# Retention and feed-forward on one core: no limit on the loads under way, and other places for rows 8 to 11

## The chip, the cores and the metric

The kernel runs on one core of one Trainium2 chip. The metric is the device time of one execution in microseconds. The core has five engines that each take their own instructions in order: PE (matrix products; its weight loads are listed apart as PEld), DVE (vector), ACT (scalar), POOL and SP. SP issues nearly all DMA transfers here; 16 DMA engines carry them. SBUF is the memory on the core, PSUM the banks into which PE writes, HBM the large memory outside.

## What is computed

A retention layer (an attention whose state decays by a constant per head) is followed by a feed-forward layer with a hard-swish product. The reference, cut to what matters:

```python
# q, k, v: (4, 8, 768, 64); w_in: (512, 2048); w_out: (2048, 512)
gamma = 1.0 - 2.0 ** (-5.0 - np.arange(H, dtype=np.float32))
for t in range(S):
    state = gamma[None, :, None, None] * state + np.einsum('bhd,bhe->bhde', k[:, :, t], v[:, :, t])
    y[:, :, t] = scale * np.einsum('bhd,bhde->bhe', q[:, :, t], state)
x = y.transpose(0, 2, 1, 3).reshape(B * S, H * D)      # 3072 tokens x 512
h = x @ w_in
g = h * np.clip(h + 3.0, 0.0, 6.0) / 6.0
return g @ w_out
```

## The kernel before

**Tiling.** The 3072 tokens are 24 rows of 128. Four rows (one block of 128 time steps of each of the four batches) make a unit of 512 tokens, so there are six units. The kernel has two phases. In the first, the retention of a row gives a 128 x 512 piece of x; with the four pieces of a unit, sixteen tiles of the first feed-forward product follow, one for each block of 128 columns of `w_in`; each result `g` is written to HBM (`gd`). In the second phase (from about 300 us) `g` is read back and multiplied by `w_out`, in a form that needs seven products for eight. To keep float32 accuracy, each operand is split into a high and a low float32r part, and a product is made as high x high, high x low and low x high. One tile (`mm1_step`, line 654) is so twelve matmuls of 512 columns, and its `h` is turned into `g` by ACT (line 668) and DVE (line 671) and stored by SP (line 677).

**Weights.** `w_in` and `w_out` arrive as 64-bit words, and `convert` (line 197) makes float32 of a block of 128 x 512: SP fetches 512 KB into `st` (two buffers), ACT takes the absolute value (line 210), DVE clips, shifts and joins in four steps (lines 214, 218, 229, 235), then ACT and DVE split it into high and low (lines 261 and 165). In the first phase block j of `w_in` is needed by tile j of unit 0.

**A row.** Its four parts are `kt`, `qt`, `vn`, `kn`, 256 KB each. `load` (line 453) fetches them; `vn` is scaled by decays on ACT and POOL (rows 0 to 7: ACT line 474, for rows 0 to 3 half of it on POOL) or on POOL alone (line 471, later rows). PE then makes the scores (line 383), the product with the state carried over (line 371), the new state part (line 408) and, after DVE and ACT have masked the scores into `am` (lines 542 and 547), the inner product (line 395). DVE scales the result by `dq` (line 633) and ACT and DVE split it into x (lines 261 and 165). `burst(new, old)` (line 693) puts the scores and the state part of one row and the two `y` products of the row before it on PE together. Rows 0 to 7 have space of their own (`early`); for later rows the buffers `kt`, `kn` have one place each, `qt` and `vn` two.

**What sets the order.** PE's order is the order in which steps are added. The list `turns` (line 726) has four tiles of unit 0, then one tile of unit 0 and one of unit 1 in turn, then units 2 to 5. After each turn `advance(n)` adds bursts until n of them are there; of `retention`'s steps (line 706), the 11th is the first half of row 8, the 12th is row 9 with the second half of row 8, and so on to the 15th, row 12 with row 11. For unit 1 the line that says when is

```python
advance(2 * UR + 3 + int((jj + 1) / NF * UR + 0.5))
```

with UR = 4 and NF = 16: the 11th step behind the unit's first tile, the 12th to 15th behind its second, sixth, tenth and fourteenth (jj = 1, 5, 9, 13). On the other engines the class `Plan` (line 42) decides: each step has a cost, a rank and dependencies, and `order` (line 71) plays the program through and issues what could start first, by rank where several could. For a load it takes that it lands no sooner than FLIGHT after its issue, that transfers follow each other at RATE us for each KB, and that no load starts before the DEPTH-th last has landed. While SP still has loads of rank under -50 (the list FIRST, line 422: rows 0 to 7 and blocks 0 to 4 of `w_in`), it takes them in exactly that order. Where PE would stand idle in this play, in the first 60 us, `spin` (line 761) adds matmuls on a constant to keep PE running. The resulting order is written into the program; on the chip each engine keeps to it and waits where data come later.

**The limit.** `load_from` (line 187), used for rows, decays and weights, adds to each load a wait until the fourth load back has landed. The stores of `g` and the second phase's loads (line 812) do not use it.

Of the kernel before, what the change touches and what calls it, by code (L numbers as in the profile page):

```python
# [41 lines left out]
class Plan:  # L42


    SEEN = {"PE": 0.25, "DVE": 0.14, "ACT": 0.16, "POOL": 0.2, "SP": 0.0}
    FIRST, RATE, FLIGHT, DEPTH = 2.0, 0.00266, 2.0, 4

    def __init__(self):
        self.steps, self.boxes = [], {}
# [6 lines left out]
    def add(self, engine, cost, run, deps=(), rank=0.0, boxes=(), kb=0, port=False):  # L56
        step = Step(engine, cost, run, [d for d in deps if d], rank, self.SEEN[engine])
        step.kb, step.boxes, step.port = kb, boxes, port or engine == "POOL"
        for b in boxes:
            b.users.append(step)  # L60
        self.steps.append(step)
        return step
# [52 lines left out]
def retention_ffn(ctx: ExitStack, tc: tile.TileContext, qkv, w_in, w_out, dvs, dqs, out, B, H, S, D):  # L115
# [6 lines left out]
    nc = tc.nc  # L122
    DM, NT = out.shape
    NF = w_in.shape[0]
# [5 lines left out]
    UR = 4  # L130
# [50 lines left out]
    plan = Plan()  # L181
# [4 lines left out]

    def load_from(to, src):

        ins = nc.sync.dma_start(out=to, in_=src).ins  # L189
        if len(started) >= plan.DEPTH:  # L190
            tc.add_manual_dep(ins, started[-plan.DEPTH], behind, reason="few loads at a time")
        started.append(ins.name)

    behind = mybir.DependencyInfo(mybir.DependencyClass.Sync, mybir.DependencyReason.DATA)
    started = []

    def convert(src, rank, soon=None):

# [3 lines left out]
        def fetch():  # L202
            t["st"] = wst_tile("st", I64, 2)
            load_from(t["st"], src)
            words = t["st"].bitcast(I32).rearrange("p (n w) -> p n w", w=2)
            t["lo"], t["hi"] = words[:, :, 0], words[:, :, 1]
# [82 lines left out]
    def build_w1(j, rank):  # L289
        spans, k = [], 0  # L290
        while k < NK:
            s, o = divmod(j * NK + k, 14)
            spans.append((k, min(NK - k, 14 - o)))
            if s not in w1_boxes:
                w1_boxes[s] = place_box("w" if s else "w0")
            k += spans[-1][1]
        t, box, dep = convert(w_in[j], rank, first("w", j, rank - 3))

        def parts():
            w = t["w"].rearrange("p (k n) -> p k n", k=NK)  # L300
            for k, n in spans:
                to, o = w1_block(j, k)
                yield to[:, o : o + n, 0], to[:, o : o + n, 1], w[:, k : k + n]

        mine = [w1_boxes[(j * NK + k) // 14] for k, n in spans]
        w1_ready[j] = split_step(parts, [n * P for k, n in spans], dep, rank, (box, *mine)), mine
# [4 lines left out]
    def build_w2(n, rank):  # L311
        j, h = divmod(n, 2)
        if not h:
            w2_boxes[j] = place_box(W2[j])
        t, box, dep = convert(w_out[j, h], rank)
        sums = plan.box("ws", 1)

        def add_up():
            w = t["w"].rearrange("p (b n) -> p b n", b=4)
            t["sm"] = sm = wst.tile([P, 4, P], F32, tag="ws", name=nm("ws"))  # L320
            m12, m11, m21, m22 = (w[:, i] for i in range(4))
            dve_sub(sm[:, 1], m12, m11)
            dve_sub(sm[:, 3], m22, m12)
            dve_sub(sm[:, 2], m22, sm[:, 1])
            dve_sub(sm[:, 0], sm[:, 2], m21)

        def target():
            if j not in w2c:
                w2c[j] = place([P, 7, 2, 2, P], F32R, nm("w2"), W2[j])
            return w2c[j]  # L330

        def parts():
            to, w = target(), t["w"].rearrange("p (b n) -> p b n", b=4)
            yield to[:, 0:3, 0, h], to[:, 0:3, 1, h], w[:, 1:4]

        def more():
            to = target()
            yield to[:, 3:7, 0, h], to[:, 3:7, 1, h], t["sm"]

        both = add("DVE", 1.0, add_up, (dep,), rank, (box, sums), port=True)  # L340
        split_step(parts, [3 * P], dep, rank, (box, w2_boxes[j]))
        split_step(more, [4 * P], both, rank, (sums, w2_boxes[j]))
# [79 lines left out]
    FIRST = [(0, "vn"), ("w", 0), (0, "kt"), (0, "qt"), (0, "kn")]  # L422
# [10 lines left out]
    def load_part(x, src, o, rank):  # L433

        if o is not None:
            e, i = divmod(o, 7)
            if e not in early_boxes:
                early_boxes[e] = plan.box("wf" if e < 2 else "we", 2 if e < 2 else 3)
            box = early_boxes[e]
        else:  # L440
            box = plan.box(f"l{x}", BUFS[f"l{x}"])
        to = {}

        def fetch():
            if o is not None:
                to["t"] = early_tile(e)[:, i]
            else:
                to["t"] = apool.tile([P, NPAIR, P], F32, tag=f"l{x}", name=nm(x), bufs=BUFS[f"l{x}"])
            load_from(to["t"].rearrange("p h n -> p (h n)"), src)

        return to, box, add("SP", 0.35, fetch, tiles_done[-5:-4], rank, (box,), kb=256)
# [202 lines left out]
    def mm1_step(u, jj, at):  # L654
        h_box, g_box, t = plan.box("h", NH), plan.box("g", 3), {}

        def run():
            t["h"] = h = ps_h.tile([P, UT], F32, tag="h", name=nm("h"))
            for k in range(NK):
                w, o = w1_block(jj, k)  # L660
                for n, (a, b) in enumerate(((0, 0), (0, 1), (1, 0))):
                    nc.tensor.matmul(  # L662
                        h, w[:, o, a], xs[u][b][:, k], start=k + n == 0, stop=(k, n) == (NK - 1, 2), skip_group_check=True
                    )

        def upper():
            t["g"] = hpool.tile([P, UT], F32, tag="g", name=nm("g"))
            nc.scalar.activation(out=t["g"], in_=t["h"], func=AF.Relu, bias=three)  # L668

        def product():  # L670
            ins = nc.vector.scalar_tensor_tensor(  # L671
                out=t["g"], in0=t["g"], scalar=6.0, in1=t["h"], op0=ALU.min, op1=ALU.mult
            )
            ends.append(ins.ins)

        def store():
            nc.sync.dma_start(out=gd[jj // 2][:, u, jj % 2], in_=t["g"])

        ready, mine = w1_ready[jj]
        assert len(x_ready[u]) == UR  # L680
        one = add("PE", 2.72, run, (ready, *x_ready[u]), at, (h_box, *mine, *x_boxes[u]))
        tiles_done.append(one)
        two = add("ACT", 0.62, upper, (one,), at + 1, (h_box, g_box))
        three_ = add("DVE", 0.61, product, (two,), at + 1, (h_box, g_box))
        add("SP", 0.35, store, (three_,), at + 1, (g_box,), kb=256)
# [5 lines left out]
    at = iter(range(1 << 30))  # L691
# [27 lines left out]
    def advance(n):  # L719

        nonlocal done
        while done < min(n, NROW + 3):
            next(gen)
            done += 1
# [7 lines left out]
    for n, (u, jj) in enumerate(turns):  # L732
        while n_w1 < min(NF, jj + 2):
            build_w1(n_w1, next(at) + (W_NEXT if n_w1 else W_FIRST))
            n_w1 += 1
        if jj in WHEN.get(u, ()):
            build_w2(n_w2, next(at) + 6.0)
            n_w2 += 1
        if (u, jj) == (NU - 1, 0):
            add("PE", 0.0, lambda: swap_pools(), (), float(next(at)))  # L740
        mm1_step(u, jj, float(next(at)))
        if n < UR:
            advance(UR + 2 + n + (n == UR - 1))
        elif u == 1:
            advance(2 * UR + 3 + int((jj + 1) / NF * UR + 0.5))
        elif 1 < u < NU - 1:
            advance(UR * (u + 1) + 3 + int((jj + 1) / NF * UR + 0.5))

# [7 lines left out]
    def swap_pools():  # L756
        nonlocal late
        att.close()
        late = ctx.enter_context(tc.tile_pool(name="late", bufs=1, side="right", reuse_waits="tile"))
# [249 lines left out]
```

## Time and profile before

| | us |
|---|---|
| median of three runs | 587.72 |
| lowest and highest | 585.54, 588.31 |
| the profiled execution's own time | 588.53 |
| its span, first to last instruction | 586.7 |
| PE busy | 568.4 |
| DVE busy | 418.9 |
| ACT busy | 244.1 |

The page gives busy times for each engine, and the span in 40 slices with one digit for each slice (tenths of the slice that the engine was busy; PEclk is the granted clock of PE, also in tenths). A row of a timeline has the start, the duration, the engine, the line, and in square brackets the idle time before it and what ended it. A row of the waits says which instruction stood, what released it, the total, how often and the longest. A row with two numbers and a colon ahead is a stretch of the span, with the busy time of PE, its weight loads, DVE, ACT and POOL, the granted clock, the DMA engines' busy share, and GB/s.

The mean over the whole span hides the stages: PE's share is 97%, but the first slices differ from the rest.

### The profile page before, as it was taken

How to read it: one execution, taken by the hardware profiler on the slowest of the kernel's cores; microseconds unless marked ns; L12 is line 12 of the kernel's file. 1: busy time of each engine (PE TensorE's matmuls, PEld its weight loads, DVE VectorE, ACT ScalarE, POOL GpSimd, SP SyncE). 2: the span in 40 equal slices, each digit the busy share in tenths (PEclk: the TensorE clock that was granted, in tenths of full speed). 3: DMA queues.
4: the chain of work that ended last, by engine and by line, in shares of the span. 5: the costliest groups of instructions: out<-in, count | busy, mean ns of one | idle time of the engine just before them, and what ended most of it. 6: DMA issues, size and time to landing. Idle time of an engine off the chain costs nothing.

```text
span 586.7 us, 12760 instructions
## 1 busy us (share of the span) xinstructions
PE 568.4 (97%) x5102; PEld 467.7 (80%) x5102; DVE 418.9 (71%) x752; ACT 244.1 (42%) x442; POOL 20.9 (4%) x25
## 2 busy tenths in 40 slices
PE   7687999999999999999999999999999999999997
PEld 6566888888888888888888888888888888888885
DVE  3567898888943598443345967998689966799743
ACT  5464444544422343222234544444444344344330
POOL 1000000000010000000000000000000000000000
PEclk9899999999999999999999999999999999999999
DMA  8888557757654466455245529974789546897002
GB/s 269 251 262 285 197 190 262 250 173 258 232 205 157 168 218 233 155 193 176 92 161 185 189 94 332 384 240 121 238 285 306 177 113 190 278 320 227 1 1 107
DMA packets 61260, 119.91 MB, mean 204 GB/s; under 512 B 7057, under 2 KB 7313, under 8 KB 61201
## 3 DMA queue, kind: packets, MB, share of 16 engines
q1 hardware_dynamic: 60912, 119.04, 60.8%
q8 instruction: 40, 0.66, 0.5%
q14 instruction: 20, 0.16, 0.1%
q10 hardware_dynamic: 288, 0.06, 0.0%
HBM read 87.61 MB, written 31.46 MB: 203 GB/s over the span
## 4 chain that ended last, share of the span: by engine, by line
PE 90%; DMA 8%; DVE 1%; ACT 0%; issue 0%; SPq 0%; DVEq 0%; ACTq 0%
PE h L662 44%; PE o L848 40%; DMA early<-in_qkv 6%; DMA st<-in_w_in 3%; PE y L395 2%; PE sc L383 2%; PE y L371 1%; PE sc L408 1%; SPq L189 0%; ACT wm L210 0%; DVE am L542 0%; DVE wb L229 0%; ACT g L668 0%; ACT w L261 0%; DVE ww L235 0%
## 5 line engine op out<-in xcount | busy, mean ns | idle before, releaser
L662 PE MATMUL h<-x,w 128*128 128x512 f32 x1152 | 269.2, 393 | 0.8 <-DVE x L165 0.7
L662 PEld LDWEIGHTS h<-x,w 128*128 128x128 f32 x1152 | 215.1, 188 | 47.2 <-DVE x L165 1.1
L848 PE MATMUL o<-gc,w 128*128 128x512 f32 x1008 | 233.2, 393 | 0.0
L848 PEld LDWEIGHTS o<-gc,w 128*128 128x128 f32 x1008 | 189.3, 188 | 43.7
L671 DVE SCALAR_TENSOR_TENSOR g<-g,h 128x512 f32<-128x512 f32 x96 | 65.8, 685 | 82.1 <-ACT g L668 81.4
L668 ACT ACTIVATE g<-h,three 128x512 f32<-128x512 f32 x96 | 65.7, 686 | 113.0 <-PE h L662 112.8
L253 ACT ACTIVATE gc<-gr 128x512 fp32r<-128x512 f32 x120 | 71.5, 623 | 57.2 <-PE o L848 43.3
L165 DVE TENSOR_TENSOR gc<-gr,gc 128x512 fp32r<-128x512 f32 x120 | 79.3, 684 | 20.9 <-ACT gc L253 20.8
L253 ACT ACTIVATE gc<-keep 128x512 fp32r<-128x512 f32 x48 | 30.4, 632 | 64.4 <-PE o L848 42.2
L165 DVE TENSOR_TENSOR gc<-keep,gc 128x512 fp32r<-128x512 f32 x48 | 32.8, 685 | 12.6 <-ACT gc L253 12.5
L210 ACT ACTIVATE wm<-st 128x512 f32<-128x512 f32 x32 | 21.5, 672 | 39.8 <-DMA st<-in_w_out 19.8
L471 POOL TENSOR_TENSOR vn<-vn,cst_sb 128x512 f32<-128x512 f32 x16 | 18.2, 1137 | 245.1 <-DMA vn<-in_qkv 220.5
L261 ACT ACTIVATE x<-xr 128x512 fp32r<-128x512 f32 x24 | 15.1, 630 | 27.2 <-DVE xr L633 27.1
L214 DVE TENSOR_SCALAR wm<-wm 128x512 f32<-128x512 f32 x32 | 13.5, 422 | 15.8 <-ACT wm L210 15.7
L865 DVE SCALAR_TENSOR_TENSOR u<-o,u 128x512 f32<-128x512 f32 (+1 forms) x31 | 20.0, 664 | 6.4 <-PE o L848 6.4
L229 DVE SCALAR_TENSOR_TENSOR wb<-st,wb 128x512 int32<-128x512 int32 x32 | 23.3, 727 | 0.2
L235 DVE SCALAR_TENSOR_TENSOR ww<-st,wb 128x512 int32<-128x512 int32 x32 | 21.9, 686 | 0.3
L261 ACT ACTIVATE w<-ww 128x384 fp32r<-128x384 f32 (+2 forms) x34 | 18.5, 549 | 6.9 <-DVE ww L235 6.8
L168 DVE TENSOR_TENSOR keep<-gr,gr 128x512 f32<-128x512 f32 x24 | 16.4, 686 | 5.8 <-DMA gr<-gd 5.7
L165 DVE TENSOR_TENSOR w<-ww,w 128x384 fp32r<-128x384 f32 (+2 forms) x34 | 19.9, 590 | 0.7 <-ACT w L261 0.7
L542 DVE TENSOR_TENSOR am<-sc,mask 128x512 f32<-128x512 f32 (+1 forms) x26 | 16.5, 641 | 3.4 <-ACT am L547 2.2
L165 DVE TENSOR_TENSOR x<-xr,x 128x512 fp32r<-128x512 f32 x24 | 16.5, 687 | 3.1 <-ACT x L261 2.3
(52 smaller groups left out, 335.0 us busy)
## 6 DMA issues: line engine op xcount, KB each, us to landing
gr<-gd SPq DMA_DIRECT2D x168, 256.0 KB, 4.3
gd<-g SPq DMA_DIRECT2D x96, 256.0 KB, 2.6
early<-in_qkv SPq DMA_DIRECT2D x32, 256.0 KB, 4.5
st<-in_w_in SPq DMA_DIRECT2D x16, 512.0 KB, 4.2
st<-in_w_out SPq DMA_DIRECT2D x16, 512.0 KB, 3.9
kt<-in_qkv SPq DMA_DIRECT2D x16, 256.0 KB, 4.0
qt<-in_qkv SPq DMA_DIRECT2D x16, 256.0 KB, 4.3
vn<-in_qkv SPq DMA_DIRECT2D x16, 256.0 KB, 4.9
```

The lines of the kernel that those rows point to most:

```text
L165: return nc.vector.tensor_tensor(out=out_, in0=a, in1=b, op=ALU.subtract)
L210: nc.scalar.activation(out=t["m"], in_=t["hi"].bitcast(F32), func=AF.Abs)
L229: nc.vector.scalar_tensor_tensor(out=b, in0=t["hi"], scalar=-0x40000000, in1=b, op0=ALU.bitwise_and, op1=ALU.bitwise_or)
L235: nc.vector.scalar_tensor_tensor(out=t["w"].bitcast(I32), in0=t["lo"], scalar=29, in1=t["b"], op0=ALU.logical_shift_right, op1=ALU.bitwise_or,
L253: nc.scalar.activation(out=hi, in_=src, func=AF.Copy)
L261: nc.scalar.activation(out=hi, in_=src, func=AF.Copy)
L471: nc.gpsimd.tensor_tensor(out=v, in0=v, in1=scale[:, :, None].to_broadcast([P, hs.stop - hs.start, D]), op=ALU.mult)
L662: nc.tensor.matmul(h, w[:, o, a], xs[u][b][:, k], start=k + n == 0, stop=(k, n) == (NK - 1, 2), skip_group_check=True)
L668: nc.scalar.activation(out=t["g"], in_=t["h"], func=AF.Relu, bias=three)
L671: ins = nc.vector.scalar_tensor_tensor(out=t["g"], in0=t["g"], scalar=6.0, in1=t["h"], op0=ALU.min, op1=ALU.mult)
L848: nc.tensor.matmul(banks[b, i, h], w2c[jj][:, RIGHT[i], a, h], gc[:, q, c], start=jj == 0 and n == 0, stop=jj == NFP - 1 and n == 2, skip_ ...
L865: nc.vector.scalar_tensor_tensor(out=out_[:, cut], in0=banks[b, i, h][:, cut], scalar=f, in1=other[:, cut], op0=ALU.mult, op1=ALU.add)
```

## The change

The limit in `load_from` goes, with the list that it kept; the planner's constants become FLIGHT 2.2 and DEPTH 9; and for unit 1 the bursts are put behind other tiles.

```diff
-    FIRST, RATE, FLIGHT, DEPTH = 2.0, 0.00266, 2.0, 4
+    FIRST, RATE, FLIGHT, DEPTH = 2.0, 0.00266, 2.2, 9
...
     def load_from(to, src):

-        ins = nc.sync.dma_start(out=to, in_=src).ins
-        if len(started) >= plan.DEPTH:
-            tc.add_manual_dep(ins, started[-plan.DEPTH], behind, reason="few loads at a time")
-        started.append(ins.name)
-
-    behind = mybir.DependencyInfo(mybir.DependencyClass.Sync, mybir.DependencyReason.DATA)
-    started = []
+        nc.sync.dma_start(out=to, in_=src)
...
         if n < UR:
             advance(UR + 2 + n + (n == UR - 1))
         elif u == 1:
-            advance(2 * UR + 3 + int((jj + 1) / NF * UR + 0.5))
+            advance(2 * UR + 3 + sum(jj >= x for x in (4, 7, 10, 13)))
```

With the new line the 11th step stays behind the first tile of unit 1; the 12th to 15th come behind its fifth, eighth, eleventh and fourteenth (jj = 4, 7, 10, 13). The loads of a row are added with its burst and wait for the fifth-last tile step added by then, so they move along.

## The prediction

> **What bounds the kernel now.** I read the slices of the whole span first, then who PE waited for, then the busy time by stage, then SP's waits and the landing times. The page's slices:
>
> ```profile
> PE   7687999999999999999999999999999999999997
> PEclk9899999999999999999999999999999999999999
> DMA  8888557757654466455245529974789546897002
> GB/s 269 251 262 285 197 190 262 250 173 258 232 205 157 168 218 233 155 193 176 92 161 185 189 94 332 384 240 121 238 285 306 177 113 190 278 320 227 1 1 107
> ```
>
> A slice is 14.7 us. PE is full from the fifth slice to the last; only the first four, about 59 us, have room. The waits of PE up to 140 us (total, times, longest):
>
> ```profile
> PE sc L383 <- DMA early<-in_qkv: 4.6, 2, 2.6
> PE sc L383 <- ACT x L261: 2.5, 1, 2.5
> PE y L395 <- DVE am L542: 1.6, 2, 1.3
> PE idle L348 <- DVE warm L345: 1.5, 1, 1.5
> PE sc L383 <- ACT wm L210: 1.4, 1, 1.4
> PE y L371 <- DVE xr L633: 1.1, 1, 1.1
> PE sc L408 <- DMA early<-in_qkv: 1.0, 1, 1.0
> PE h L662 <- DVE x L165: 0.7, 1, 0.7
> ```
>
> That is all: 14.4 us, of which 1.5 is the start. The landmarks are unit 0's first tile at 27.98 and its fifth at 59.27, from the timeline of PE (start, duration):
>
> ```profile
> 21.78 0.69 PE L408 MATMUL sc<-early 64*64 64x64 f32 x32 [1.03 <-DMA early<-in_qkv]
> ...
> 27.98 0.58 PE L662 MATMUL h<-x,w 128*128 128x512 f32 x1
> ...
> 59.27 6.61 PE L662 MATMUL h<-x,w 128*128 128x512 f32 x24
> ...
> 66.91 5.74 PE L662 MATMUL h<-x,w 128*128 128x512 f32 x24
> ```
>
> Busy time of each engine by stage, with granted clock, DMA share and GB/s at the end of the row:
>
> ```profile
> 2.00:27.98 25.98, 19.03 (x428) 17.18 (x427) 11.58 (x22) 13.98 (x45) 2.46 (x4) 0.93 0.85 273
> 27.98:59.27 31.29, 25.03 (x516) 20.05 (x514) 23.03 (x42) 16.59 (x45) 1.58 (x2) 0.97 0.81 273
> 59.27:142.18 82.91, 82.91 (x909) 68.63 (x905) 72.25 (x142) 39.77 (x65) 4.66 (x4) 0.99 0.66 220
> 142.18:300.00 157.82, 157.82 (x1998) 130.86 (x1998) 90.14 (x171) 50.27 (x79) 11.95 (x11) 1.00 0.54 183
> 2.00:46.20 44.20, 34.97 (x757) 29.83 (x757) 23.03 (x42) 23.66 (x76) 2.46 (x4) 0.96 0.85 276
> 352.00:381.00 29.00, 29.00 (x127) 23.54 (x126) 24.10 (x40) 13.27 (x22) 0.00 (x0) 1.00 1.01 357
> ```
>
> (The five busy times are PE, its weight loads, DVE, ACT, POOL.) From 59.27 to 300 PE is busy every microsecond, so nothing the change does there can win. The opening is fed at 276 GB/s with the DMA engines 0.85 busy; at 352 to 381 us, where the loads have no hand-written limit, the same engines carried 357 GB/s at a share of 1.01. What holds the opening's loads back stands in SP's waits up to 60 us and in the landing times (of `early` loads, then of the second phase's `gr` loads, with their SP wait):
>
> ```profile
> SPq L189 <- DMA early<-in_qkv: 15.7, 28, 2.4
> SPq L189 <- DMA st<-in_w_in: 10.1, 6, 3.0
> SPq L189 <- DVE ww L235: 8.2, 2, 4.9
> ```
> ```profile
> DMA to landing us min/median/max: 2.6/4.4/6.7
> ```
> ```profile
> DMA to landing us min/median/max: 2.6/4.3/7.5
> ```
> ```profile
> SPq L812 <- DMA gr<-gd: 14.9, 31, 1.8
> ```
>
> SP stood 25.8 us waiting for earlier loads to land: that is the wait on the fourth load back. So the opening is bound by four loads under way, with engines in planned order behind it.
>
> **The change, step by step.** *Limit removed.* All loads up to w_in block 4 have ranks below -50 and go out in a fixed order, so only the limit, and the two `st` buffers, pace them. In the 44.2 us to 46.2, when that block lands, 276 GB/s x 44.2 = 12.2 MB moved. At 357 GB/s this takes 34.2 us, 10.0 less; if instead the present rate is only scaled to a full share, 276 / 0.85 = 325 GB/s, it takes 37.5, 6.7 less. These are my two ends for the stream: 15% to 23% shorter. No instruction is added.
>
> What is late next at SP is the `st` pair: block 3 may be fetched only after block 1 was joined (the kind of wait in the 8.2 us row). In the fetch order between blocks 1 and 3 stand rows 4 and 5, a `dq` and block 2: 11 pieces of 256 KB, 2.9 MB, 8 us at 357 GB/s. The conversion itself, ACT's first step to DVE's join:
>
> ```profile
> 23.75 0.66 ACT L210 ACTIVATE wm<-st 128x512 f32<-128x512 f32 x1 [0.77 <-DMA st<-in_w_in]
> ```
> ```profile
> 27.87 0.69 DVE L235 SCALAR_TENSOR_TENSOR ww<-st,wb 128x512 int32<-128x512 int32 x1
> ```
>
> It takes 28.56 - 23.75 = 4.8 us, inside those 8, so I cost this wait at nothing; without the cover it would hold back rows 6 and 7 by up to the difference. Stores of `g` queue behind more loads: nothing, since each has the three `g` buffers and tiles here are over 5 us apart.
>
> *First tile.* It follows row 3, whose gather waited for its load until 21.78. That load is 19.8 us into the stream, so it comes 15% to 23% of that, 3.0 to 4.5 us, earlier. The chain from there to 27.98 (6.2 us) stays. I take 3.7: first tile at 24.3.
>
> *First to fifth tile.* 31.29 us now, PE busy 25.03, DVE 23.03. The data set one lower end (block 4 at 46.2 less 6.7 is 39.5, and its conversion ended 7.2 us after landing, from these two rows, so 46.7):
>
> ```profile
> 46.19 0.66 ACT L210 ACTIVATE wm<-st 128x512 f32<-128x512 f32 x1 [3.18 <-DMA st<-in_w_in]
> ```
> ```profile
> 52.74 0.68 DVE L165 TENSOR_TENSOR w<-ww,w 128x512 fp32r<-128x512 f32 x1
> ```
>
> The engines set a later one: PE 25.0 us; DVE, at the occupancy of 72.25 / 82.91 = 0.87 that it holds beside a full PE in the next stage, 23.03 / 0.87 = 26.4. So DVE, not the load, becomes the bound. I take 27.5, a microsecond above it, since ACT and DVE run in a planned order that reality will not match. Ends: 25.0 and 28.5. Fifth tile at 24.3 + 27.5 = 51.8, a gain of 7.5.
>
> *Clock.* The 24 matmuls at 59.27, after the last waits, took 6.61 us, the 24 at 66.91 took 5.74: 0.87 us of slow clock. With fewer waits ahead I count 0.5 of it; ends 0 and 0.9.
>
> *Planner constants.* Depth 9 and flight 2.2 change only the planned order on ACT, DVE, POOL and SP (PE's is written out). The plan already assumed one 256 KB piece per 0.68 us, and reality was slower; now it comes closer. I count nothing beyond the microsecond above; ends are the rivals below.
>
> *Rows 8 to 11.* Row 8's scores stay behind the first tile of unit 1; row 9's (with row 8's second half) move from behind that unit's second tile to its fifth, row 10's from the sixth to the eighth, row 11's from the tenth to the eleventh, row 12's stay at the fourteenth. PE's instruction count does not change. Between bursts there are then 8, 6, 6 and 4 tiles instead of 2, 8, 8 and 6. Each row brings four 256 KB loads on SP and one POOL step with it, later by as much; they pass `g` stores and `st` fetches on SP's queue. From 142.18 to 300 bursts stand every four tiles, and PE has no idle time, so such spacing costs nothing; six is easier. DVE gains slack at 60 to 75 us, exactly where the pulled-in opening needs it for w_in blocks 5 and 6. Taken as 0; ends -2 (blocks late for their tile) and 0.
>
> **Sum.** The profiled execution took 588.53 us (span 586.7). 588.53 - 3.7 - 3.8 - 0.5 = 580.5. The median of the runs is 587.72, 0.8 lower, so against it I forecast **579.7**. Its own range: gains from 3.0 + 2.8 + 0 - 2.0 = 3.8 to 4.5 + 6.3 + 0.9 = 11.7, so 576.0 to 583.9.
>
> **Rivals.**
> 1. *The limit is not what binds* (no change, 587.7). The shortest load took 2.6 us; if that were the trip of each, four of 262 KB per 2.6 us are 403 GB/s, more than the 357 seen, and a fifth load would only stand in line. Against: the median is 4.4, the share 0.85, and SP waited 25.8 us. Something else could also hold the number down: the `gr` loads have no limit in the code and still waited 31 times for an earlier one. But 357 GB/s x 4.3 us is 1.54 MB, about six loads under way, so such a hold lies above four. The Trainium skill, "DMA: Bandwidth & Descriptors", section "Anatomy of one DMA", puts a DMA at about 2.0 us fixed plus its bytes at 436 GB/s. By it a 256 KB load takes 2.6 us, four under way suffice, and the time would stay near 587.7; the shortest landing here agrees, the median of 4.4 does not. Chance 0.10.
> 2. *The planned order binds.* Loads come earlier, the first tile gains 3.0, but the 31.29 us from there stay, because ACT and DVE each take their next step in the planned order. For it: the largest PE wait, 2.5 us, is on an ACT step behind a conversion. Against: that ACT step itself stood behind a late `st` load. 587.7 - 3.0 = 584.7. Chance 0.14.
> 3. *Slower.* The planner, told of nine loads under way, puts a conversion's first ACT step ahead of a row's mask copy although the block lands later, and ACT stands. Place: blocks 1 to 4, between the first and the fifth tile. Price: each like the 2.5 us wait, 10, against the 2.5 + 1.4 that PE has now through ACT, so 6.1 more: 593.8. It decides when landings run further behind the plan than now, that is if the deep queue moves less than 276 GB/s. The 357 GB/s row speaks against. Chance 0.07.
> 4. *More than forecast*: idle time and filler matmuls both go, under 576. Chance 0.04.
>
> **How the numbers follow.** The forecast has 0.65. The range 575.5 to 586.0 holds it, rival 2 and most of 4; it leaves out 1 and 3 and a little else, under 0.2. A difference of 0.5%, 2.9 us, is about what a measurement of this kernel can tell from no change. Faster by more: 0.65 + 0.04 + half of rival 2 = 0.76. Within: 0.07 + 0.10 = 0.17. Slower by more: 0.07.
>
> **What would show it.** Right: DMA share near 1 and over 320 GB/s to about 40 us; no SP wait of L189 on an `early` load above a few us in total; first tile near 24, fifth near 52; PE idle in front of it under 8 us; no idle time afterwards. Wrong: the same fifth tile with longer landings (rival 1); ACT idle on `st` as long as now (2, 3); PE idle on w_in blocks after the fifth tile, or at a moved burst. The second phase should not move.

## The result and the profile after

The changed kernel takes 583.1 us in the median (580.43 to 584.08), the kernel before 586.67 in the runs beside it: the ratio of the mean times is 0.9923, with a 95% interval of 0.9895 to 0.9951 (the two medians alone give 0.9939). The forecast was 579.7 within 575.5 to 586.0. The direction holds, and the time lies in the range; of the gain of 8.0 us there came 3.6 between the medians, 4.5 between the means, and 4.4 between the two profiled executions (spans 586.7 and 582.3).

The slices of the page, as for the kernel before:

```profile
PE   7699999999999999999999999999999999999997
PEclk9699999999999999999999999999999999999999
DMA  9685587676744576554255439974789546897002
GB/s 324 260 298 193 180 282 262 190 274 228 236 146 163 197 225 221 175 178 168 75 181 181 163 118 350 373 226 130 255 260 314 178 110 196 281 312 223 1 4 105
```

PE is now full from the third slice on instead of the fifth, but its clock in the second slice has fallen from 8 to 6 tenths. The waits of PE up to 140 us (total, times, longest; after 60 us there is none):

```profile
PE sc L377 <- DMA early<-in_qkv: 2.8, 3, 1.4
PE sc L402 <- issue: 2.7, 1, 2.7
PE sc L377 <- issue: 2.3, 1, 2.3
PE idle L342 <- DVE warm L339: 1.5, 1, 1.5
PE h L656 <- DVE x L165: 0.6, 1, 0.6
PE y L389 <- issue: 0.4, 1, 0.4
PE y L365 <- DVE xr L627: 0.3, 1, 0.3
PE pace L355 <- issue: 0.3, 1, 0.3
```

The waits through ACT and DVE are nearly gone, and two new ones stand in front: 2.7 and 2.3 us "<- issue", time in which PE waited for nothing that the profile shows. Busy time by stage (PE, its weight loads, DVE, ACT, POOL; granted clock, DMA share, GB/s), with the first tile at 30.04 and the fifth at 55.73:

```profile
2.00:30.04 28.04, 20.22 (x428) 17.66 (x427) 11.64 (x22) 14.09 (x46) 2.45 (x4) 0.82 0.82 302
30.04:55.73 25.69, 24.02 (x516) 19.54 (x514) 21.97 (x42) 17.40 (x46) 1.04 (x1) 1.00 0.72 258
55.73:138.10 82.37, 82.37 (x909) 68.31 (x907) 74.51 (x148) 39.36 (x65) 4.37 (x4) 1.00 0.69 233
2.00:14.60 12.60, 9.75 (x221) 8.57 (x219) 5.57 (x10) 6.99 (x23) 1.84 (x3) 1.00 1.03 373
14.60:23.30 8.70, 3.74 (x126) 3.56 (x126) 1.98 (x3) 2.35 (x7) 0.61 (x1) 0.69 1.04 392
23.30:30.04 6.74, 6.73 (x81) 5.53 (x82) 4.09 (x9) 4.76 (x16) 0.00 (x0) 0.63 0.15 54
```

From the first to the fifth tile it takes 25.69 us instead of 31.29, better than forecast. The loads run at 373 and 392 GB/s up to 23.3 us, above both ends that the forecast had, and then nearly stop (54 GB/s up to 30.04). But the first tile, forecast at 24.3, comes at 30.04, later than before. SP's waits up to 60 us show that the loads are not without a limit now:

```profile
SPq L189 <- DVE ww L229: 19.8, 4, 9.9
SPq L189 <- DMA early<-in_qkv: 9.1, 23, 0.9
```

SP still waits 23 times for an earlier `early` load. Counted from the issues and landings in the trace, at most eight of SP's transfers are under way at any time, and most of the loads go out as the eighth load back lands. So the change raised four to eight; "no limit" below means that none is written in `load_from`. What sets the eight no run shows.

Why the first tile is late the timeline of PE says (start, duration, count; idle time before it in brackets):

```profile
13.69 0.89 PE L377 MATMUL sc<-early 64*64 64x128 f32 x29 [0.71 <-DMA early<-in_qkv]
16.85 0.33 PE L377 MATMUL sc<-early 64*64 64x64 f32 x3 [2.27 <-issue]
16.98 0.69 PE L402 MATMUL sc<-early 64*64 64x64 f32 x32
17.46 1.09 PE L389 MATMUL y<-am,early 64*64 64x128 f32 x32
18.26 1.57 PE L377 MATMUL sc<-early,early 64*64 64x128 f32 x32
19.54 1.05 PE L402 MATMUL sc<-early 64*64 64x64 f32 x27
23.31 0.38 PE L402 MATMUL sc<-early 64*64 64x64 f32 x3 [2.72 <-issue]
...
30.04 0.58 PE L656 MATMUL h<-x,w 128*128 128x512 f32 x1
...
55.73 5.74 PE L656 MATMUL h<-x,w 128*128 128x512 f32 x24
```

Both stops fall inside a group of equal matmuls whose data are there: 29 of row 2's 32 scores run, then nothing for 2.3 us, then the last three. Between the stops lie 3 + 32 + 32 + 32 + 27 = 126 matmuls and as many weight loads, 252 instructions, with a few others about 256. That number has a meaning on the page, in the rows on the instruction queues (packets, MB, share) and, for the stretch from 14 to 15 us, in the same view of the transfers:

```profile
q8 instruction: 40, 0.66, 0.5%
```
```profile
q8 instruction: 1, 0.02, 6.7%
```

0.66 MB in 40 packets is 16.4 KB a packet. If a packet holds 256 instructions, 40 of them hold 10,240, and PE has 5102 + 5102 instructions besides a few others. So PE's program comes in blocks of 256 instructions over the same 16 DMA engines as the loads. Narrow windows put the start of single packets at 14.2, 20.9 and 24.4 us, and a DMA engine is busy 1.1 to 1.3 us with each; PE goes on 1.5 and 1.3 us after the end of the first two. The Trainium skill, "Runtime: NRT & Kernel Launch", section "Instruction fetch mechanics", says that the sequencer refills in blocks of 16 KiB over its own DMA queue while it executes, and that the cost of a boundary is mostly hidden. The block size agrees with these rows; that it is hidden does not, here.

Theory A, then: with a long queue of loads the instruction packet gets its turn late, and the short matmuls of rows 1 to 3 use a block up before the next is there. Theory B: a fetch is always that slow, and showed less before only because PE stood waiting for data anyway. Theory C: it is no fetch at all, but a data wait that the profile does not name.

### The profile page after: what moved, and what is told of

The parts are those of the page before. It is cut to its first block, busy times and chain, and to the rows that moved or that the text cites. A ratio compares the mean times of both kernels' runs of the same rounds, so it can differ in the third digit from the quotient of the medians.

```text
span 582.3 us, 12762 instructions
## 1 busy us (share of the span) xinstructions
PE 567.6 (97%) x5102; PEld 467.0 (80%) x5102; DVE 420.3 (72%) x752; ACT 245.3 (42%) x442; POOL 19.7 (3%) x25
## 4 chain that ended last, share of the span: by engine, by line
PE 95%; DMA 2%; issue 1%; DVE 1%; SPq 0%; DVEq 0%
PE h L656 46%; PE o L842 40%; PE y L389 3%; PE sc L377 3%; PE sc L402 2%; DMA early<-in_qkv 2%; PE y L365 2%; PE spin L758 0%; SPq L189 0%; DVE wb L223 0%; PE pace L355 0%; DVE ww L229 0%; DVE xr L627 0%; DVE x L165 0%; DVE u L859 0%
## 5 line engine op out<-in xcount | busy, mean ns | idle before, releaser
L465 POOL TENSOR_TENSOR vn<-vn,cst_sb 128x512 f32<-128x512 f32 x16 | 16.9, 1058 | 244.4 <-DMA vn<-in_qkv 219.5
L165 DVE TENSOR_TENSOR w<-ww,w 128x384 fp32r<-128x384 f32 (+2 forms) x34 | 22.1, 656 | 0.8 <-ACT w L255 0.7
L168 DVE TENSOR_TENSOR keep<-gr,gr 128x512 f32<-128x512 f32 x24 | 16.4, 685 | 7.0 <-DMA gr<-gd 7.0
```

What stands on the lines that cost most here:

```text
L165: return nc.vector.tensor_tensor(out=out_, in0=a, in1=b, op=ALU.subtract)
```

## The experiments

**The parts of the change alone.** First the limit's end with the planner's constants, the bursts at their old tiles:

```diff
-            advance(2 * UR + 3 + sum(jj >= x for x in (4, 7, 10, 13)))
+            advance(2 * UR + 3 + int((jj + 1) / NF * UR + 0.5))
```

> No limit on the loads and the planner's new constants, but the rows 8 to 11 at their old tiles. Both theories of PE's two stalls keep them here: 2.3 and 2.7 us at the same two places, about 14.6 and 20.6 us, first tile at 30, fifth near 55.7 us. If the moved rows are worth nothing, as the prediction had it, the time is that of the changed kernel, 0.992 of before within 0.003. If the moved rows carry part of the gain, PE shows idle time between 56 and 80 us and the ratio is nearer to 1.

Measured: 583.35 us, ratio 0.9935 (0.9912 to 0.9958); stalls of 2.3 and 3.7 us at the same two places, first tile at 29.7, fifth at 54.9 us, and after it only 0.3 us of idle time. Then the moved rows alone, in the kernel before:

> The old limit of four and the old planner constants, only the rows 8 to 11 at their new tiles. If the moved rows are worth nothing: the time of before, ratio 1.000 within 0.003, first tile at 28.0 and fifth at 59.3 us. If they carry the gain: the fifth tile stays at 59.3 and the ratio is below 0.996.

Measured: 585.84 us, ratio 0.9976 (0.9948 to 1.0003); the first tile at 28.0, but the fifth at 55.5 and not at 59.3. The moved rows come after the fifth tile in PE's order, so a direct effect is not to be expected. Openings with the limit of four differ: from the first tile to the fifth 31.3 us in the profiled execution of before, 27.4 here and 33.8 in the next kernel. With one profile of each, program and execution are not told apart. The moved rows are not told from nothing. Third, planner and rows as changed, but the limit of four kept on every load:

```diff
     def load_from(to, src):

-        nc.sync.dma_start(out=to, in_=src)
+        ins = nc.sync.dma_start(out=to, in_=src).ins
+        if len(started) >= 4:
+            tc.add_manual_dep(ins, started[-4], behind, reason="few loads at a time")
+        started.append(ins.name)
```

> The changed kernel with the limit of four kept on all loads: only the planner's constants and the moved rows are changed. If the gain from the first to the fifth tile (31.3 us before, 25.7 after) comes from the limit's end: 29 to 31 us here, PE waits behind conversions as before, ratio 0.996 to 1.000. If it comes from the planner's order: 26 to 27 us here, ratio 0.990 to 0.993.

Measured: 588.13 us, ratio 1.0004 (0.9983 to 1.0026); from the first tile (27.1) to the fifth (60.9) 33.8 us, more than the 29 to 31 expected. PE waits on DVE again and on data:

```profile
PE y L371 <- DVE xr L633: 3.7, 1, 3.7
PE sc L383 <- DMA early<-in_qkv: 3.5, 4, 2.1
PE sc L383 <- DVE am L542: 3.0, 2, 2.1
```

So the new constants and the moved rows win nothing while the limit stands, and the gain between first and fifth tile needs the limit's end. The limit's end with the old constants was not run: whether the new planner order helps it along is not shown.

**Do the stalls sit at a count of instructions?** The changed kernel with 22 matmuls fewer in the warm-up:

```diff
-    for n in range(WARM):
-        nc.tensor.matmul(idle[:, 0:P], warm[:, 0], warm[:, 1], start=True, stop=True)
+    for n in range(3):
+        nc.tensor.matmul(idle, warm[:, 0], warm.rearrange("p a n -> p (a n)"), start=True, stop=True)
```

> The changed kernel, but the 14 warm-up products of 128 columns (28 matmuls in the trace) are 3 of 512 columns (6 matmuls): 22 matmuls and 22 weight loads fewer ahead of everything. If the stalls sit at every 256th instruction of PE (theories A and B), both move by 22 matmuls: from behind the 29th score of row 2 to about the 19th of its state products (line 402), and from behind the 27th state product of row 3 to about the 17th matmul of the inner product that follows (line 389). If they hang on data or on the place in the row (theory C), they stay in the scores of row 2 and the state products of row 3.

Measured: both moved as theories A and B said. One timeline row each side of the stop; of the 32 state products of row 2, 18 run before it, of the 32 inner products 17 (two stand in a row of their own ahead):

```profile
13.69 0.55 PE L402 MATMUL sc<-early 64*64 64x64 f32 x18
16.41 0.59 PE L402 MATMUL sc<-early 64*64 64x64 f32 x12 [2.18 <-issue]
...
20.03 0.61 PE L389 MATMUL y<-am,early 64*64 64x128 f32 x15
22.14 0.56 PE L389 MATMUL y<-am,early 64*64 64x128 f32 x15 [1.49 <-issue]
```

One execution gave 581.17 us. Counted in matmuls from the start of the program, the stops of the changed kernel stand behind the 221st and the 347th, and here, within one, as well. The next boundary but one shows too, at the 600th: 0.38 us in the changed kernel, ahead of a group of 32 inner products, and 0.58 us here, with ten of that group left. Theory C falls. The other way round, 76 matmuls more:

```diff
-    for n in range(WARM):
+    for n in range(10):
         nc.tensor.matmul(idle[:, 0:P], warm[:, 0], warm[:, 1], start=True, stop=True)
+    for n in range(42):
+        nc.tensor.matmul(idle[0:64, 0:4], warm[0:64, 0, 0:64], warm[0:64, 0, 0:4], start=True, stop=True)
```

> The changed kernel with 76 matmuls more in the warm-up (10 of the old ones and 42 tiny products, 104 matmuls in the trace instead of 28), all before row 0's data are there. It adds instructions and no data. Theory A or B with blocks of 256: every boundary falls 76 matmuls earlier. The first now lies inside the warm-up, so its block is fetched before the queue is long; the one that gave the first stall now lies in row 1's state products (about the 19th) and finds its block there: no stall in row 2's scores. The next falls at about the 15th to 19th matmul of row 1's inner product and may still stall, 1 to 3 us. Together 1 to 3 us of stalls instead of 4.6 to 5.0, first tile at 25.5 to 27.5, time 580 to 582. If the stalls had another cause (theory C), they stay where they were, and the longer warm-up only costs.

Measured: 583.44 us, ratio 0.9939 (0.9919 to 0.9960). The stall in row 2's scores is gone; one of 1.6 us is left, at the forecast place, behind the 16th matmul of row 1's inner product:

```profile
19.79 0.56 PE L391 MATMUL y<-am,early 64*64 64x128 f32 x16
21.95 0.56 PE L391 MATMUL y<-am,early 64*64 64x128 f32 x16 [1.59 <-issue]
```

The price was missed: the tiny products took some 70 ns each, the warm-up ended near 12 us, and row 0's scores, at 7.6 before, began at 11.7. The first tile came at 29.4, later than the 25.5 to 27.5 expected, the fifth at 54.5. With the limit of six (below) as well:

> The longer warm-up with the limit of six for the first 19 loads. Theory A: both measures act on the same stalls, so the second boundary stalls less than with the longer warm-up alone, under 1.5 us; first tile at 25.5 to 27, time 579.5 to 581.5.

Measured: 584.55 us, ratio 0.9959 (0.9942 to 0.9976), a stall of 3.7 us at the same place, not under 1.5, and the first tile at 32.2 us, not at 25.5 to 27. The limit ended at load 19, before that boundary; the same shows in the next runs.

**Queue or fetch alone?** The changed kernel with the limit of four on the first 19 loads only (`if 4 <= len(started) < 19:` in the diff above), then with six:

> The changed kernel with the limit of four kept for the first 19 loads (to row 3 and weight block 1), none after. Theory A (PE's instruction blocks stand in line behind the queued loads): the instruction packets start 1 to 2 us after the block boundary instead of 3.9, no stall over 1.5 us inside a group of matmuls, first tile at 27 to 28, fifth at 53 to 54 us, time about 2 us below the changed kernel (ratio to before 0.988). Theory B (a fetch is that slow without any queue, and shows only because the data are early): with the data later again the stalls hide behind data waits, first tile at 28; the packets still start about 3.9 us after the boundary. Theory C (neither, a data wait that the profile does not name): the stall stays near 2.5 us at both places.

Measured: 581.69 us, ratio 0.9907 (0.9877 to 0.9937). No stall over 0.6 us is left; PE waits for data instead:

```profile
PE sc L383 <- DMA early<-in_qkv: 4.8, 3, 2.2
```

First tile at 27.6, fifth at 53.2 us. The changed kernel was run again beside the kernels that follow:

> The changed kernel once more, as the mark for the three others on this chip: ratio 0.992 within 0.003, PE's stalls of 2 to 3 us at the same two places.

Measured: 582.39 us, ratio 0.9918 (0.9890 to 0.9947), stalls of 2.6 and 2.0 us, first tile at 27.9, fifth at 53.55. With stalls nearly as long its profiled execution is 2.1 us shorter than the first one (spans 580.2 and 582.3): from the end of the first stop to the first tile the clock was 0.85 here and 0.61 there. The stalls cost their length, and in some of the profiled executions slow matmuls behind them.

> The limit of six for the first 19 loads, none after. Theory A: the instruction packets wait between the two cases, 2 to 3 us behind the boundary; data of rows 2 and 3 come 1 to 2 us earlier than with four, and the stalls are under 1.5 us each; first tile at 26.5 to 28, time 580 to 582. If a queue of six is already as long for the packets as one without limit: stalls of 2 us or more, first tile near 29, time of the changed kernel.

Measured: 582.36 us, ratio 0.9923 (0.9893 to 0.9953), stalls of 0.6 and 5.1 us, first tile at 29.6. At the first boundary the expectation held; the second was worse than without a limit, and the first tile came as late as the other branch of the expectation had it. The two with the shorter warm-up:

> The limit of four for the first 19 loads and the shorter warm-up together. No stall without cause over 1 us; rows 2 and 3 still wait for data as with the limit of four alone, so the first tile stays at 27 to 28 and the time at 581 to 582: the shorter warm-up helps only where the stalls are.

Measured: 581.37 us, ratio 0.9903 (0.9872 to 0.9934), no stall over 0.4 us, first tile at 27.3.

> The limit of six for the first 19 loads and the shorter warm-up. Data as early as with six, block boundaries 22 matmuls later. Theory A: stalls under 1.5 us each, behind the 20th state product of row 2 and the 17th inner product of the same row; first tile at 26 to 27, time 579.5 to 581.5, the lowest of all if the shift and the shorter queue add.

Measured: 581.27 us, ratio 0.9902 (0.9874 to 0.9930), no stall at the first boundary, one of 2.1 us at the second, not under 1.5 (and 0.5 at the 600th matmul), first tile at 27.3, later than the 26 to 27 expected. Against the changed kernel none of these four is told apart by its time.

To see the queue itself I take the moment when PE crosses into a block as that when the block after it is asked for. This is inferred, from the position of the stops; no row shows the request. From there to the start of the packet, us, beside the number of SP's transfers under way at that moment, counted as above:

| kernel | under way | first boundary | second |
|---|---|---|---|
| changed | 8, 8 | 3.9 | 4.0 |
| changed, again | 8, 8 | 4.5 | 3.5 |
| limit's end, old rows | 8, 8 | 4.0 | 3.8 |
| shorter warm-up | 8, 8 | 3.7 | 3.3 |
| six on 19 loads | 6, 8 | 2.9 | 5.5 |
| six on 19, shorter warm-up | 6, 8 | 2.2 | 3.6 |
| before | 4, 4 | 1.1 | 1.7 |
| moved rows alone | 4, 4 | 2.1 | 3.0 |
| four on all loads | 4, 4 | 2.0 | 2.2 |
| four on 19 loads | 4, 4 | 1.6 | 2.6 |
| four on 19, shorter warm-up | 4, 5 | 2.7 | 0.3 |
| longer warm-up | 8, 8 | 1.5 | 2.5 |
| longer warm-up, six on 19 | 6, 7 | 0.2 | 4.7 |

Down to the last two rows the order is clear: 3.3 to 5.5 us beside eight, 2.2 to 2.9 beside six, up to 3.0 beside four or five. The longer warm-up does not fit, with 1.5 and 2.5 beside eight. Waits of 0.2 and 0.3 us say that the crossing need not be the moment of the request, so single values are rough. The third packet is open: in the changed kernel, again and with the old rows it waited 1.1, 1.2 and 1.1 us beside five transfers with no new one behind them, with the shorter warm-up 3.1 us, also beside five. A fetch that takes about 4 us whatever else is under way (theory B) does not fit the rows with four. In the runs with six the limit had ended when the second block was asked for, so the last kernel keeps six up to load 25, with the shorter warm-up:

```diff
-        if 6 <= len(started) < 19:
+        if 6 <= len(started) < 25:
```

> The limit of six for the first 25 loads (to row 4, not only row 3) and the shorter warm-up. Theory A: with the queue kept short past the second boundary, its instruction packet starts under 3 us behind it (3.7 to 5.5 where the limit ended at load 19), stall under 1.5 us, first tile at 26 to 27, time 579.5 to 581.5. If the queue does not matter (theory B): the second stall stays at about 2.

Measured: 579.16 us (579.07 to 580.72), ratio 0.9867 (0.9842 to 0.9892), faster than before. Against the changed kernel, which was not run beside it, the ratios to before point the same way (0.9923 and 0.9918 there, with intervals from 0.9895 and 0.9890 up); from the limit of six that ends at load 19 (0.9902) it is not told apart. Around the two stops and the two tiles:

```profile
13.85 0.55 PE L408 MATMUL sc<-early 64*64 64x64 f32 x18
15.73 0.40 PE L408 MATMUL sc<-early 64*64 64x64 f32 x12 [1.34 <-issue]
...
18.39 0.64 PE L395 MATMUL y<-am,early 64*64 64x128 f32 x17
20.53 0.56 PE L395 MATMUL y<-am,early 64*64 64x128 f32 x15 [1.50 <-issue]
...
25.11 0.58 PE L662 MATMUL h<-x,w 128*128 128x512 f32 x1
...
50.73 5.76 PE L662 MATMUL h<-x,w 128*128 128x512 f32 x24
```

Row 2's state products start as early as without limit (13.85), the stops are 2.8 us together instead of 5.0, and PE's clock up to 26 us is 1.00. The two packets started 2.8 and 2.5 us behind their boundaries, with six transfers under way at both, under 3 as theory A said; the second stop is 1.5 us, at the edge of what it allowed. First tile at 25.1, earlier than expected, fifth at 50.7: the forecast for the change had said 24.3 and 51.8.

## Why the prediction was right in its direction and too large

**What bounds the kernel** was right: the profiled executions differ by 4.4 us in span and by 4.4 at the end of the 24 matmuls at the fifth tile, no run shows PE idle behind that tile for more than 0.3 us, and with the limit kept the gain is zero. But SP's wait for earlier loads did not go: on `early` loads it fell from 15.7 to 9.1 us, where one of the signs of being right had named a few us, since eight under way took the place of four. Rival 1 had reckoned with such a hold above four.

**The stream** ran faster than forecast up to 23.3 us, 373 to 392 GB/s against 325 to 357. It then broke off, at the place that the working named and costed at nothing, and block 4 landed at 42.1 us by the trace, not at 36.2 to 39.5. The fetch of weight block 3 waited 9.9 us for block 1 to be joined; SP's timeline, and what ACT did ahead of block 1's conversion:

```profile
20.30 0.33 SPq L189 DMA_DIRECT2D early<-in_qkv  x1
30.62 0.33 SPq L189 DMA_DIRECT2D st<-in_w_in  x1
```
```profile
23.84 0.45 ACT L572 ACTIVATE state<-sc 128x128 f32<-128x128 f32 x2 [2.98 <-PE sc L402]
24.17 0.67 ACT L204 ACTIVATE wm<-st 128x512 f32<-128x512 f32 x1
```

The cover of 8 us for a conversion of 4.8 did not hold, since ACT came to the conversion only after row 3's state, which stood behind PE's second stall. For the stream that cost was not nothing; for PE it was: after 14 us PE waits for no load.

**The first tile** is the step that failed, "first tile at 24.3", a gain of 3.7. The load itself came as forecast: the last of row 3 landed at 17.6 us by the trace, against 21.6 before, a gain inside the 3.0 to 4.5. But the step took that load for the only thing that came earlier or later, and carried the rest over unchanged. The runs show a second user of the DMA engines, PE's own instructions. With eight loads under way instead of four their packets started about 4 instead of about 2 us behind the boundary: 4.6 to 5.0 us of stalls in the two profiles of the changed kernel, and slow matmuls behind them. In the first that turns a gain of 3.7 into -2.1, in the second into 0.1. The row of the instruction queue was on the page before too, in its third part.

**From the first to the fifth tile** the forecast of 27.5 us measured 25.7, near PE's own 24.0; DVE at 21.97 of 25.69 us is 0.86 busy, the occupancy assumed, so the microsecond added for the planned order was not needed. The gain was 5.6 instead of 3.8, but both are reckoned from the 31.29 us of one execution; two other kernels with the limit of four took 27.4 and 33.8.

**The clock**: the 24 matmuls at the fifth tile take 5.74 us, so 0.87 was won where 0.5 was counted. **The sum**: -2.1 + 5.6 + 0.9 = 4.4 us, where 3.7 + 3.8 + 0.5 = 8.0 was forecast. The first tile missed its own range of 3.0 to 4.5; that the time still lies in the whole range is in part luck, since the stretch after it won 1.8 us more than counted. **Moved rows and planner constants** at nothing: not told from nothing with the limit in place.

**Rival 1** is out by 0.9923; the fit that the prediction sets beside it is given in that section of the Trainium skill for transfers issued by POOL, while these loads are issued by SP. **Rival 2** came the other way round: it let the first tile gain 3.0 and the stretch after it stay, and its 584.7 lies near the result by luck. **Rival 3** did not come: ACT's idle time on `st` loads up to 60 us fell from 13.4 to 0.4 us.

## What to carry to other kernels

Here PE's instructions came over the same DMA engines as data. Where many short matmuls run beside a deep queue of loads, look for a stop "<- issue" inside a group of equal instructions, and count the instructions between two such stops. A limit on loads under way may be worth keeping for just the stretch in which instructions are used up fast; the best kernel here did so, though it is not told apart from its neighbour with a shorter stretch. When a written limit goes, count what is under way: here another of eight stood behind it. And a stage's length taken from one profiled execution has a spread that belongs in the range.

## What the runs showed of the hardware that was not expected

In the changed kernel a block of 256 PE instructions took 6.5 us from the crossing of the boundary before it to its use (10.3 to 16.85, 16.85 to 23.31) with the DMA engines at a share above 1, against the 3.7 us in which PE worked through such a block at 0.65 of its clock (16.85 to 20.6). The packet itself kept an engine busy for 1.1 us. The granted clock behind a stop was not the same each time, with the program unchanged: 0.50 from 23.3 to 26.0 us behind a stop of 2.7 us, and in the second profile 0.61 from 16.8 to 20.5 behind one of 2.6, but 1.00 from 22.8 on behind one of 2.0. Among ten executions of the changed kernel spans of 582.3 us at a mean clock of 0.988 and of 578.6 at 1.000 occur. What decides stayed open.
